# k^T v on both partition halves: ScalarE copies across the halves in place of an exchange by products

## The chip, the core and the metric

One core of a Trainium2 chip runs the whole kernel. The metric is device time in microseconds (us); the kernel before takes 374.31 us, the median of 3 runs (373.65 to 374.38). Engines are named as in the profile: PE is TensorE (PEld its weight loads), ACT is ScalarE, DVE is VectorE, POOL is GpSimd, SP is SyncE, which here only issues DMAs.

## The reference

Two blocks follow each other. The first is linear attention over 8 batches, 8 heads, 576 positions and head size 64:

```python
kv = np.einsum('bhsd,bhse->bhde', k, v)
out = np.einsum('bhsd,bhde->bhse', q, kv)
rms = np.sqrt(np.mean(out * out, axis=-1, keepdims=True) + 1e-06)
attn = (out / rms * g_norm)
x = attn.transpose(0, 2, 1, 3).reshape(4608, 512)
```

The second is a mixture of 8 experts with an early exit: tokens with `x @ w_skip > 0` go to the expert with the largest `x @ w_gate`, which adds `gate * (relu(x @ w1[e]) @ w2[e])` to x; the others leave as they are. Everything is float32.

## The kernel before

**Two stages.** The attention stage (lines 141 to 1057) takes the first 118 us of the profiled execution: it loads q, k and v, makes x, stores it, and works out the routing beside that. The expert stage (from line 1060) takes the rest: each expert's tokens are gathered, and two layers are computed with large products.

**The state of a batch.** For each batch b, `state` (L372) sums k^T v of its 8 heads in PSUM, in 64x64 products (L380) cut into portions over several steps. The heads are numbered 2u+w; those of w=0 stand on partitions 0 to 63 of `sum_ps`, those of w=1 on partitions 64 to 127. Two positions are handled together: q^T has an even position's 64 dimensions on partitions 0 to 63 and an odd position's on 64 to 127. So every head's k^T v must stand in the tile `kvd` twice, once on each half of the partitions, with zeros beside it. The copy on the head's own half is called `own(b, w)`. Each row holds 146 columns (PK): 9 gate columns, 128 columns of k^T v of two heads, 9 gate columns; the gate columns hold k^T v times the gate and skip weights, so that logits come out of the same product as x.

The steps that make `kvd` are:

- the end of `state`: two ACT copies of 64x256 (L387) put k^T v of `sum_ps` on its own half
- `state_t` (L390): four products with the identity (L394) turn it, and one ACT copy (L397) takes the result to `kvT`
- `state_m` (L400): two products (L403) with the gate weights, and two ACT copies of 64x36 (L406) put the gate columns on the own half
- `state_s` (L408), the exchange: two products with the identity (L412), each of which reads one half of `kvd` and writes the other half of PSUM, and two ACT copies of 64x292 (L416) that put all 146 columns of two heads on the other half of `kvd`

A float32 product shows in the profile as two passes, so the exchange is 4 rows of PE in each batch, 32 in all.

**The order.** It is written out by hand: all engines get their instructions in program order. A loop over 36 units and two more steps (L1014) runs, in step n: `turn(n+1)` (transposes of q, L461, and an ACT copy to `qT`, L464), `root(n-1)` (ACT square root, L530), the jobs called "early", `values(n)` (products of q with `kvd`, L499, into a PSUM tile `o_ps`, ahead of them the transposes of a last position, L480; then an ACT square, L515), the jobs "mid", `norm(n-1)` (DVE reciprocal, L537, and DVE product L546, which reads `o_ps` and ends its use), `squares(n)` (DVE sum, L523), and the jobs "pe". From unit 30 on `squares(n)` comes before `norm(n-1)`. The portions of `state` and the three other steps of batch b are such jobs, laid out in L964 to L982: `state_t` in step s, `state_m` in step s too (as "pe", so after `values`), `state_s` in step s+1. For the last batch the places differ somewhat. Batch 0 is done ahead of the loop (L954 to L962).

**What is shared.** `o_ps` has two buffers, so `values(n)` waits until L546 has read unit n-2. `sum_ps` has one, and the next batch's `state` waits until it has been read; units 30 and 33 use its room too. The results of L394, L403 and L412, and the routing's products (L694, L700, L922), lie in one PSUM bank, `g_ps`. Units 16, 17, 34 and 35 (L509) do the ninth position of four batches together.

**Loads.** k, v and q of a batch come in four pieces each (`load_part`, L118), 288 KB a piece, all issued by SP in program order, with stores of x between them. k and v have 3 buffers, q has 2.

Of the kernel before, what the change touches and what calls it, by code (L numbers as in the profile page):

```python
# [17 lines left out]
def kernel(  # L18
# [43 lines left out]
    nc = tc.nc  # L62
    B, H, S, D = q.shape
# [10 lines left out]
    G = E + 1  # L74
# [4 lines left out]
    PK = 2 * KD  # L79

    KVD = 5
# [28 lines left out]
    g_ps = ps_g.tile([P, 512], FP32)  # L110
# [17 lines left out]
    def load_kv(b, js=range(4)):  # L128
        if b < B:
            if js.start == 0:  # L130
                for name, to in (("k", kts), ("v", vts)):
                    to[b] = kv_pool.tile([P, 4, C, D], FP32, tag=name, name=name)
            for j in js:
                for src, t in ((k, kts[b]), (v, vts[b])):
                    load_part(t, src, b, j)

    def load_q(b):
        if b < B:
            qts[b] = load(q_pool, "q", q, b)
# [61 lines left out]
    ident = keep.tile([P, P], FP32)  # L201
# [3 lines left out]
    kvds = []  # L205
# [27 lines left out]
    for a in range(2):  # L233
        r = slice(a * 64, (a + 1) * 64)
# [60 lines left out]
    for lo, m, _ in runs:  # L295
# [26 lines left out]
        out=srow[:, :].rearrange("p (r c) -> p r c", c=CK),  # L322
# [33 lines left out]
    def own(b, w):  # L356

        return kvds[b % KVD][w * 64:(w + 1) * 64, :, w, w, :]

    sum_all = ps_kv.tile([P, 2, 512], FP32, name="sum_ps")  # L360
    sum_ps = sum_all[:, :, 0:2 * D].rearrange("p a (u d) -> p a u d", u=2)
    sw_ps = g_ps[:, 0:2 * PK]
    kvT_ps = g_ps[:, 0:2 * P].rearrange("p (u x) -> p u x", u=2)
    lg_ps = g_ps[:, 2 * PK:2 * PK + 8 * G].rearrange("p (u a w g) -> p u a w g", u=2, a=2, w=2)

    def ends_of(x):

        ap = [list(d) for d in x.ap]
        assert ap[-1] == [1, PK]
        return bass.AP(x.tensor, x.offset, ap[:-1] + [[PK - G, 2], [1, G]])  # L370

    def state(b, some):  # L372

        kt, vt = kts[b], vts[b]
        for i in some:
            u, c = divmod(i, C)
            for w in range(2):
                for a in range(2):
                    r = slice(a * 64, (a + 1) * 64)
                    nc.tensor.matmul(  # L380
                        out=sum_ps[w * 64:(w + 1) * 64, a, u, :],
                        lhsT=kt[r, 2 * u + w, c, :], rhs=vt[r, 2 * u + w, c, :],
                        start=(c == 0), stop=(c == C - 1), skip_group_check=True)
        if some.stop < 2 * C:
            return
        for w in range(2):
            nc.scalar.copy(out=own(b, w)[:, :, G:G + 2 * D].rearrange("p u (a d) -> p a u d", a=2),  # L387
                           in_=sum_ps[w * 64:(w + 1) * 64, :, :, :])

    def state_t(b):  # L390
        for u in range(2):
            for w in range(2):
                r = slice(w * 64, (w + 1) * 64)
                nc.tensor.matmul(out=kvT_ps[:, u, r], lhsT=kvds[b % KVD][:, u, w, w, G:G + 2 * D],  # L394
                                 rhs=ident[:, r], start=True, stop=True)
        kvT = att_pool.tile([P, 2, P], FP32, tag="kvT", name="kvT", bufs=1)
        nc.scalar.copy(out=kvT[:, :, :], in_=kvT_ps)  # L397
        kvTs[b] = kvT

    def state_m(b):  # L400
        kvT = kvTs.pop(b)
        for u in range(2):
            nc.tensor.matmul(out=lg_ps[:, u, :, :, :], lhsT=kvT[:, u, :], rhs=gw_b[:, u, :, :, :],  # L403
                             start=True, stop=True)
        for w in range(2):
            nc.scalar.copy(out=ends_of(own(b, w)), in_=lg_ps[w * 64:(w + 1) * 64, :, :, w, :])  # L406

    def state_s(b):  # L408

        for w in range(2):  # L410
            r, o = slice(w * 64, (w + 1) * 64), slice((1 - w) * 64, (2 - w) * 64)
            nc.tensor.matmul(out=sw_ps[o, :], lhsT=ident[r, r], rhs=own(b, w), start=True, stop=True,  # L412
                             skip_group_check=True)
        for w in range(2):
            o = slice((1 - w) * 64, (2 - w) * 64)
            nc.scalar.copy(out=kvds[b % KVD][o, :, w, 1 - w, :],  # L416
                           in_=sw_ps[o, :].rearrange("p (u k) -> p u k", u=2))


    units = []  # L420
# [22 lines left out]
    def at(step, part, job):  # L443
        todo.setdefault((step, part), []).append(job)
# [7 lines left out]
    def turn(n):  # L452
        _, b, i, u = units[n]
        if i is None:
            qTs[n] = q8s[b][:, u, :, :, :]
            return
        ps = ps_q.tile([P, 2, 2, 2, 64], FP32, tag="q", name="q_ps")
        for w in range(2):
            for hf in range(2):
                c = 4 * i + 2 * hf  # L460
                nc.tensor.transpose(out=ps[:, w, :, hf, :], in_=qts[b][:, 2 * u + w, c:c + 2, :],  # L461
                                    identity=ident[:, :])
        qT = att_pool.tile([P, 2, 2, P], FP32, tag="qT", name="qT")
        nc.scalar.copy(out=qT[:, :, :, :].rearrange("p w a t -> p (w a t)"),  # L464
                       in_=ps[:, :, :, :, :].rearrange("p w a h t -> p (w a h t)"))
        qTs[n] = qT
# [478 lines left out]
    for b in range(KNOWN // S // 4 * 4, KNOWN // S):  # L945
        nc.gpsimd.dma_start(
            out=out[b * S:(b + 1) * S, :].rearrange("(p c) d -> p c d", c=C)[:, C - 1, :],
            in_=zero)

    starts = {}  # L950
    for n, (_, b, i, _) in enumerate(units):
        if i is not None:
            starts.setdefault(b, n)
    state(0, range(C))  # L954
    dense(4)
    state(0, range(C, 2 * C))
    dense(5)
    state_t(0)
    turn(0)
    state_m(0)  # L960
    turn(1)
    state_s(0)  # L962

    portions = {1: (1, (10, 8)), 2: (4, (6, 6, 6)), 3: (7, (5, 6, 7)), 4: (11, (5, 6, 7)),  # L964
                5: (16, (8, 4, 3, 3)), 6: (20, (4, 4, 5, 5)), 7: (24, (4, 4, 5, 5))}
    over = 0
    for b, n in starts.items():
        if b:
            step, counts = portions[b]
            i = 0  # L970
            for count in counts:
                at(step, "early" if step in (starts[1], starts[2], starts[4] - 2) else "pe",
                   lambda b=b, some=range(i, i + count): state(b, some))
                i += count
                step += 1
            assert i == 2 * C and step < n and step - len(counts) > over - 1
            last = b == B - 1
            at(step, "mid" if last else "early", lambda b=b: state_t(b))
            at(*((step + 1, "early") if last else (step, "pe")), lambda b=b: state_m(b))
            at(step + 1, "early" if step + 1 == n else "pe", lambda b=b: state_s(b))  # L980
            over = step
        at(over, "end", lambda b=b: load_kv(b + 3, range(4 if b else 2)))  # L982

        at(n + 2, "end", lambda b=b: load_q(b + 2))
        if b == 0:
            at(n + 2, "end", lambda: load_kv(3, range(2, 4)))
# [73 lines left out]
    with tc.tile_pool(name="wpool_b", bufs=1, reuse_waits="tile") as wpool_b, \  # L1060
# [526 lines left out]
        with tc.If(n_rounds > 1):  # L1587
            with tc.For_i(1, n_rounds, 1):
# [8 lines left out]
                    out=left[:, :].rearrange("p (r c) -> p r c", c=CK),  # L1597
# [39 lines left out]
```

## Time and profile before

| what | value |
|---|---|
| median of 3 runs | 374.31 us |
| profiled execution, its own time | 371.14 us |
| its span in the profile | 369.3 us |
| granted TensorE clock, mean | 0.997 |
| PE busy | 359.9 us (97%) |
| L380, k^T v: PE rows | 1152, 25.3 us |
| L499, q times `kvd`: PE rows of the 128x146 form | 240, 36.0 us |
| L412, exchange: PE rows | 32, median 431 ns |
| L387, k^T v to its own half: ACT rows | 16, median 371 ns |
| L406, gate columns: ACT rows | 16, median 186 ns |
| L416, exchange: ACT rows | 16, median 397 ns |

The profile shows one execution. A row's duration is that of one instruction from start to end; on PE rows overlap, so the distance between starts and not the duration is what a row takes of the engine. A view of the timeline merges neighbouring instructions of one line, and gives start, length and count. The chain of waits is followed back from the last instruction: at each step to what released it, or to the instruction before it on its engine. A wait that names several engines is put down to the one that came last.

### The profile page before, as it was taken

The numbers are of one execution on the slowest core, as the hardware profiler recorded it, in microseconds if no ns is written. First come the engines' busy times: TensorE is split into PE (matmuls) and PEld (weight loads), VectorE is DVE, ScalarE is ACT, GpSimd is POOL, SyncE is SP. The second block draws the span as 40 slices with busy tenths as digits, with TensorE's granted clock in tenths as the row PEclk, the third lists the DMA queues.
The fourth block names the chain that finished last, engine by engine and source line by source line (L and its number), as shares of the span: only waits on it lengthen the run. The fifth ranks groups of instructions, "written<-read, shape, count | busy, mean of one in ns | idle before, by whom it ended". The sixth has DMA issues, their size and how long they took to land.

```text
span 369.3 us, 9717 instructions
## 1 busy us (share of the span) xinstructions
PE 359.9 (97%) x3859; PEld 314.8 (85%) x3859; DVE 242.8 (66%) x630; ACT 146.2 (40%) x398; POOL 118.9 (32%) x189
## 2 busy tenths in 40 slices
PE   8999999899999999999999999999999999999994
PEld 4788998798889769599879988988998988999983
DVE  3355557767878662866847675776776876868831
ACT  2467677666777032134203511421530430441420
POOL 8036466655777072223031303303203202002003
PEclk9999999999999999999999999999999999999998
DMA  8999999999588449973617355564662772601001
GB/s 267 397 390 390 399 397 382 386 379 344 187 296 309 115 129 369 395 234 112 227 56 251 87 208 177 183 231 105 240 230 56 263 244 52 251 3 46 13 1 54
DMA packets 32808, 81.71 MB, mean 221 GB/s; under 512 B 3242, under 2 KB 3250, under 8 KB 32756
## 3 DMA queue, kind: packets, MB, share of 16 engines
q1 hardware_dynamic: 28944, 69.48, 53.0%
q0 software_dynamic: 3792, 11.53, 9.3%
q8 instruction: 32, 0.52, 0.5%
q14 instruction: 20, 0.16, 0.1%
q10 hardware_dynamic: 20, 0.02, 0.0%
HBM read 66.80 MB, written 14.48 MB: 220 GB/s over the span
## 4 chain that ended last, share of the span: by engine, by line
PE 86%; issue 5%; DMA 2%; ACT 2%; DVE 2%; POOL 1%; SPq 0%; POOLq 0%; DVEq 0%; ACTq 0%
PE bank L1261 45%; PE bank L1193 9%; PE o_ps L499 8%; PE sum_ps L380 5%; PE bank L1181 4%; PE q_ps L461 4%; DMA v<-in_v_dram 2%; PE g_ps L394 2%; PE bank L1162 2%; PE g_ps L412 1%; PE o_ps L480 1%; PE g_ps L857 1%; ACT sq L515 1%; PE g_ps L403 1%; PE q_ps L857 1%
## 5 line engine op out<-in xcount | busy, mean ns | idle before, releaser
L1271 ACT COPY p<-bank 128x128 f32<-128x128 f32 (+6 forms) x70 | 20.8, 297 | 99.0 <-PE bank L1261 97.5
L1261 PE MATMUL bank<-xt,w 128*128 128x128 f32 (+5 forms) x336 | 55.5, 288 | 0.0
L1392 POOL DMA_INDIRECT out_dram<-xg,rows x14 | 14.0, 999 | 118.1 <-DVE xg L1389 106.9
L616 POOL TENSOR_TENSOR xb<-xl,g_b 128x512 f32<-128x512 f32 x34 | 41.3, 1215 | 29.2 <-DVE rs L537 27.3
L1261 PEld LDWEIGHTS bank<-xt,w 128*128 128x128 f32 x336 | 47.0, 190 | 1.9 <-DVE bank L1265 1.4
L1265 DVE TENSOR_TENSOR bank<-bank,p 128x128 f32<-128x128 f32 (+6 forms) x70 | 23.6, 337 | 30.3 <-PE bank L1261 29.1
L499 PE MATMUL o_ps<-kvd,qT 128*128 128x146 f32 x240 | 36.0, 290 | 0.9 <-issue 0.7
L1261 PE MATMUL bank<-xs,s 128*128 128x128 f32 (+5 forms) x224 | 36.7, 288 | 0.0
L523 DVE TENSOR_REDUCE rs<-sq 128x8 f32<-128x512 f32 x36 | 24.5, 682 | 14.8 <-ACT sq L515 14.8
L499 PEld LDWEIGHTS o_ps<-kvd,qT 128*128 128x128 f32 x240 | 31.6, 189 | 1.6 <-issue 0.9
L1261 PEld LDWEIGHTS bank<-xs,s 128*128 128x128 f32 x224 | 31.1, 190 | 1.0 <-ACT p L1271 0.8
L1193 PE MATMUL bank<-w,ht 128*32 128x128 f32 (+2 forms) x424 | 29.9, 313 | 0.0
L546 DVE TENSOR_TENSOR xl<-o_ps,rs 128x584 f32<-128x584 f32 x32 | 24.5, 767 | 4.3 <-DVE rs L537 0.5
L1193 PEld LDWEIGHTS bank<-w,ht 128*32 128x32 f32 (+2 forms) x424 | 18.2, 119 | 10.7 <-issue 7.6
L1261 PE MATMUL bank<-t,ht 128*128 128x256 f32 x112 | 27.0, 384 | 0.0
L1261 PE MATMUL bank<-w,ht 128*128 128x256 f32 x112 | 26.5, 380 | 0.0
L515 ACT ACTIVATE sq<-o_ps 128x512 f32<-128x512 f32 x34 | 20.3, 597 | 15.0 <-PE o_ps L499 14.8
L1153 POOL DMA_INDIRECT xg<-out_dram,src x14 | 14.1, 1006 | 35.4 <-DMA out_dram<-xg,rows 18.6
L380 PE MATMUL sum_ps<-v,k 64*64 64x64 f32 x1152 | 25.3, 222 | 0.2 <-DMA v<-in_v_dram 0.2
L1261 PE MATMUL bank<-t,hs 128*128 128x256 f32 x112 | 25.3, 379 | 0.0
L380 PEld LDWEIGHTS sum_ps<-v,k 64*64 64x64 f32 x1152 | 21.6, 134 | 3.6 <-issue 0.9
L1261 PEld LDWEIGHTS bank<-t,ht 128*128 128x128 f32 x112 | 20.8, 190 | 3.9 <-issue 1.2
(224 smaller groups left out, 677.1 us busy)
## 6 DMA issues: line engine op xcount, KB each, us to landing
w<-in_moe_w_dram SPq DMA_DIRECT2D x16, 2048.0 KB, 10.2
k<-in_k_dram SPq DMA_DIRECT2D x32, 288.0 KB, 6.2
v<-in_v_dram SPq DMA_DIRECT2D x32, 288.0 KB, 6.5
q<-in_q_dram SPq DMA_DIRECT2D x32, 288.0 KB, 5.7
out_dram<-xb SPq DMA_DIRECT2D x29, 256.0 KB, 5.5
out_dram<-xb POOLq DMA_DIRECT2D x7, 256.0 KB, 5.9
xg<-out_dram,src POOLq DMA_INDIRECT x16, 3.5
out_dram<-xg,rows POOLq DMA_INDIRECT x16, 6.4
```

What stands on the lines that cost most here:

```text
L380: nc.tensor.matmul(out=sum_ps[w * 64:(w + 1) * 64, a, u, :], lhsT=kt[r, 2 * u + w, c, :], rhs=vt[r, 2 * u + w, c, :], start=(c == 0), stop ...
L461: nc.tensor.transpose(out=ps[:, w, :, hf, :], in_=qts[b][:, 2 * u + w, c:c + 2, :], identity=ident[:, :])
L499: mm = nc.tensor.matmul(out=ps[:, w, 0:2 * PK].rearrange("p (r k) -> p r k", r=2)[:, :, cols], lhsT=qT[:, w, a, :], rhs=kvds[b % KVD][:, u ...
L515: nc.scalar.activation(out=sq[:, :, :, :], in_=heads(ps, G, G + 2 * D), func=ACT.Square)
L523: nc.vector.tensor_reduce(out=rs[:, :, :], in_=sq[:, :, :, :].rearrange("p x y (a d) -> p x (y a) d", a=2), axis=AX.X, op=ALU.add)
L546: nc.vector.tensor_tensor(out=xl[:, :, :, :].rearrange("p x y (a k) -> p x (y a) k", a=2), in0=ps[:, :, 0:2 * PK].rearrange("p x (h k) -> ...
L616: late.append((lambda eng: eng.tensor_tensor(out=xb[:, :, 4 * u * D:(4 * u + 4) * D].rearrange("p r (w x) -> p r w x", w=2), in0=xl[:, :, ...
L1181: nc.tensor.matmul(out=hps[:, cols], lhsT=w_sb[r][0][:, dc, f * P:(f + 1) * P], rhs=xt[:, dc, cols], start=(dc == 0), stop=(dc == DC - 1))
L1193: nc.tensor.matmul(out=yps[q * m:(q + 1) * m, 0:n], lhsT=ht(f)[:, off:off + m], rhs=w_sb[r][1][:, f, q * n:(q + 1) * n], start=(f == 0), s ...
L1261: nc.tensor.matmul(out=out, lhsT=lhsT(i), rhs=rhs(i), start=start and i == 0, stop=i == k - 1, skip_group_check=True)
L1265: nc.vector.tensor_tensor(out=to, in0=x, in1=y, op=ALU.add)
L1271: nc.scalar.copy(out=t, in_=x)
```

## The change

The exchange goes. `own` gets a counterpart `other`, the same heads on the other half of the partitions, and both halves are filled by ACT copies straight out of PSUM; the copies for `other` read one half of the partitions and write the other half.

- The 64x256 copies of k^T v are made twice: for `own` where they were, at the end of `state`; for `other` in `state_t`, behind the copy to `kvT`.
- The 64x36 copies of the gate columns are made twice, both in `state_m`.
- `state_s` with its 2 products and 2 copies of 64x292 is gone from each batch, and so are its jobs.
- `state_m` is a "mid" job now and not a "pe" job (but for the last batch, where it stays "early" of the next step).

```diff
+    def other(b, w):
+        return kvds[b % KVD][(1 - w) * 64:(2 - w) * 64, :, w, 1 - w, :]
+
+    def put_sums(b, half):
+        for w in range(2):
+            nc.scalar.copy(out=half(b, w)[:, :, G:G + 2 * D].rearrange("p u (a d) -> p a u d", a=2),
+                           in_=sum_ps[w * 64:(w + 1) * 64, :, :, :])
...
-    sw_ps = g_ps[:, 0:2 * PK]
...
-        for w in range(2):
-            nc.scalar.copy(out=own(b, w)[:, :, G:G + 2 * D].rearrange("p u (a d) -> p a u d", a=2),
-                           in_=sum_ps[w * 64:(w + 1) * 64, :, :, :])
+        put_sums(b, own)
...
         nc.scalar.copy(out=kvT[:, :, :], in_=kvT_ps)
+        put_sums(b, other)
         kvTs[b] = kvT
...
-        for w in range(2):
-            nc.scalar.copy(out=ends_of(own(b, w)), in_=lg_ps[w * 64:(w + 1) * 64, :, :, w, :])
-
-    def state_s(b):
-        for w in range(2):
-            r, o = slice(w * 64, (w + 1) * 64), slice((1 - w) * 64, (2 - w) * 64)
-            nc.tensor.matmul(out=sw_ps[o, :], lhsT=ident[r, r], rhs=own(b, w), start=True, stop=True,
-                             skip_group_check=True)
-        for w in range(2):
-            o = slice((1 - w) * 64, (2 - w) * 64)
-            nc.scalar.copy(out=kvds[b % KVD][o, :, w, 1 - w, :],
-                           in_=sw_ps[o, :].rearrange("p (u k) -> p u k", u=2))
+        for half in (own, other):
+            for w in range(2):
+                nc.scalar.copy(out=ends_of(half(b, w)), in_=lg_ps[w * 64:(w + 1) * 64, :, :, w, :])
...
-    state_s(0)
...
-            at(*((step + 1, "early") if last else (step, "pe")), lambda b=b: state_m(b))
-            at(step + 1, "early" if step + 1 == n else "pe", lambda b=b: state_s(b))
+            at(*((step + 1, "early") if last else (step, "mid")), lambda b=b: state_m(b))
```

## The prediction

> **What bounds it now.** I read the page first, then busy times by stretch, then the chain of waits through the attention stage, then the timelines of ACT, DVE, PE and SP around one batch.
>
> ```profile
> span 369.3 us, 9717 instructions
> ...
> PE 359.9 (97%) x3859; PEld 314.8 (85%) x3859; DVE 242.8 (66%) x630; ACT 146.2 (40%) x398; POOL 118.9 (32%) x189
> ...
> DMA  8999999999588449973617355564662772601001
> ```
>
> PE is busy throughout, and DMA is full for the first ten slices of 9.2 us: in that time two resources can each hold the other. By stretch (PE, PEld, DVE, ACT, POOL busy; clock; DMA share):
>
> ```profile
> 20.00:30.00 10.00, 9.81 (x213) 8.85 (x203) 5.25 (x10) 5.94 (x16) 4.98 (x10) 1.00 1.05 388
> 40.00:50.00 10.00, 10.00 (x175) 9.23 (x174) 5.04 (x10) 7.62 (x21) 5.77 (x11) 1.00 1.03 394
> 90.00:100.00 10.00, 9.98 (x176) 9.13 (x174) 8.82 (x25) 7.96 (x21) 7.32 (x12) 1.00 0.57 197
> ```
>
> ACT has 2 to 4 us of 10 left; until 90 us the DMA share is at its top. The chain of waits is PE nearly without a break, and the exchange is on it. Batch 2's:
>
> ```profile
> 39.89 0.21 PE g_ps L412
> 40.10 0.17 PE sum_ps L380 x5
> 40.27 0.25 PE g_ps L412 x2
> 40.53 0.70 PE sum_ps L380 x38
> 41.22 0.34 PE o_ps L480 x2
> ```
>
> **Removed from PE.** From 39.89 to 41.22 are 1.33 us, with a portion of 48 passes of L380 in it. Such a portion alone takes 0.86 us in the chain (31.87 to 32.73), so the exchange takes 0.47. In the same way batch 3 gives 1.22 - 40/48 x 0.86 = 0.50, batches 5 and 6 give 1.10 - 0.57 = 0.53 each. Batch 1 gives 1.41 - 0.86 = 0.55, and 0.18 that L412 waits for L406 (27.25 to 27.43): 0.7. Batch 7 has no L380 beside it: 0.64. Batch 0 is followed below. Batch 4's exchange (60.8) lies where the chain runs over DVE, from the square at 59.53 to L546 at 65.61 and L480 at 66.44: nothing is gained there, and nothing lost, since DVE goes through the same work.
>
> **Added to and removed from ACT.** The timeline of ACT for batch 3:
>
> ```profile
> 45.27 0.77 ACT L387 COPY kvd<-sum_ps 64x256 f32<-64x256 f32 x2 [0.16 <-PE sum_ps L380]
> ...
> 47.00 0.37 ACT L397 COPY kvT<-g_ps 128x256 f32<-128x256 f32 x1 [0.16 <-PE g_ps L394]
> 48.12 0.60 ACT L515 ACTIVATE sq<-o_ps 128x512 f32<-128x512 f32 x1 [0.74 <-PE o_ps L499]
> 48.61 0.38 ACT L406 COPY kvd<-g_ps 64x36 f32<-64x36 f32 x2
> 49.02 0.59 ACT L464 COPY qT<-q_ps 128x512 f32<-128x512 f32 x1
> 49.50 0.30 ACT L530 ACTIVATE rs<-rs,eps_t 128x8 f32<-128x8 f32 x1
> 49.90 0.60 ACT L515 ACTIVATE sq<-o_ps 128x512 f32<-128x512 f32 x1
> 50.60 0.82 ACT L416 COPY kvd<-g_ps 64x292 f32<-64x292 f32 x2
> ```
>
> Out goes the pair of 0.82; in come a pair of 64x256 at 0.77 and one of 64x36 at 0.38: +0.33 us of ACT a batch. The copies that cross the halves have no row in the trace. The nearest rows are the same shapes without a crossing, and I take their price; bounds: that price below (nothing in a crossing could make it cheaper), twice it above (read and written as two passes).
>
> Where it lies: the pair of 0.77 starts behind L397 (47.37 to 48.14), just in ACT's idle 0.74 before the square: the square comes 0.02 later. The next batch's `state`, which waits for `sum_ps`, follows L403 on PE; for batch 2 that is 38.49, and the pair is done at 38.31. The two extra 64x36 copies delay everything behind them on ACT by 0.38 unless ACT idles before its next work. It does for batches 2, 5 and 6 (0.76, 0.64, 1.33 us idle before L464), and for batch 4 (0.47 before L530). It does not for batches 1, 3 and 7. There `qT`, the root and then DVE's L546 come later, and for L546 waits `values(n+2)`:
>
> ```profile
> 50.17 0.77 DVE L546 TENSOR_TENSOR xl<-o_ps,rs 128x584 f32<-128x584 f32 x1
> ```
>
> It ends at 50.94; L480 of unit 12, for which it frees the tile, starts at 51.51. With +0.39 it ends at 51.33, and PE, 0.50 ahead, would ask at 51.01: 0.3 of the 0.5 would go back. Batch 1 just fits (L546 of unit 3 at 29.7, asked for at 29.8).
>
> Two rules of the Trainium skill speak here. "Trace analysis" (Perfetto Trace Analysis, section Optimizing Scalar/DVE Operations) says that grouping into larger operations helps if the engine is saturated; this change cuts one copy in two. Were ACT saturated, 8 x 0.33 = 2.6 us would be lost; its rows of 5.94 to 7.96 in 10 say that it isn't, so I count only the places above. And "ScalarE: Activation LUTs" (What ACT_TABLE_LOAD costs) has neighbouring instructions overlap by about 93 ns, with 186 ns + 0.833 ns an element: the two extra 64x36 copies would cost 2 x 0.12 = 0.25. The row shows 0.38 for two, with no overlap; I take the row. The rule would give back 0.14 in each place where these copies count.
>
> **A longer hold on the shared bank.** The routing's L694 lies in `g_ps`, behind `state_m` of batch 6, and waits already (total, times, longest):
>
> ```profile
> PEld g_ps L694 <- ACT kvd L406: 0.2, 1, 0.2
> ```
>
> At 87.68 it follows the end of L406 (87.64). With four copies that is 88.03: PE, which has come to it, loses 0.4. Behind it stand L700, the transposes and `values(25)`. So batch 6 keeps 0.53 - 0.4 = 0.13.
>
> **Batch 0** is serial. ACT: `kvT` ends 13.85, the crossing pair 14.62, `qT` 15.21, the third 64x36 copy 15.8: L499 starts at 15.85, not 16.41: 0.56. **Batch 7**: the same copies push ACT's square of unit 29 from 101.37 (end) to about 101.9; DVE's sum and L902 end at 102.75 and not 102.51, and L922 needs that at 103.03 - 0.64 = 102.39: 0.36 goes back, 0.28 stays.
>
> **What is late next: the loads.** They run in a fixed order at full rate, so they don't come earlier when PE is earlier.
>
> ```profile
> 41.27 2.50 SPq L118 DMA_DIRECT2D q<-in_q_dram  x4
> ```
> ```profile
> 48.22 0.64 PE L461 MATMUL q_ps<-ident,q 128*128 128x128 f32 x4
> 51.51 0.38 PE L480 MATMUL o_ps<-ident,q 128*128 128x128 f32 x2
> ```
>
> These are the four pieces of batch 3's q, and their first use in `turn(12)`, which needs two. Issues stand 0.62 apart, and an issue of L118 lands 6.0 us later (median; 3.0 to 7.5): the second lands near 47.9, against its use at 48.44. By then PE would be 0.4 + 0.7 + 0.47 = 1.57 ahead, at 46.9. It waits; some 0.5 is left. (Batch 0's 0.56 counts as 0.4, since the last piece of batch 1's v, issued at 13.39, lands between 19.9 and 20.7 and is used at 20.74.) The wait also gives L546 of unit 10 time, so batch 3 then keeps its whole 0.5. Later loads are early by 4 us or more (batch 4's q: 53.0 + 6 for 63.7; batch 6's: 78.0 + 6 for 88.3).
>
> **Sum.** 0.5 at 48 us, +0.5 (batch 3), 0 (4), +0.53 (5), +0.13 (6), +0.28 (7) = 1.9 us. From there to the end the chain is PE, weights are fetched as their buffers come free, and all of it moves along. The profiled execution's 371.14 (span 369.3) becomes 369.2. The median of the runs stands 3.17 above that execution; the difference goes on the median: 374.31 - 1.9 = 372.4.
>
> **Rivals.** (A) As worked out: 372.4, own range 371.5 to 373.4; chance 0.48. (B) The loads don't hold PE: for it speaks that PE waited for DMA 0.2 us in all; against, the share of 1.05. Then batch 3 keeps 0.2 and the sum is 1.73 + 0.2 + 0.53 + 0.13 + 0.28 = 2.9, or 371.4; with none of the new waits at all it is 0.56 + 0.7 + 0.47 + 0.5 + 2 x 0.53 + 0.64 = 3.9, or 370.4; chance 0.2. (C) The early gains end in the loads wholly (POOL's stores, earlier too, push q of batch 3 back by up to their 0.66 us each) and the late ones in DVE, busy 8.82 of 10 behind 88 us: about -0.3, 374.0; chance 0.17. (D) Slower: crossing copies cost twice. That puts 0.77 + 0.38 more on ACT in each batch, between `kvT` and the root. For batch 3 L546 would end at 52.5, asked for at 51.0: 1.5 lost against 0.5 gained; over some five batches about +4, and 1.5 back where ACT idles: near 377. It decides from about 1.4 times the straight price, where 0.46 more a batch eats the 1.9. No row speaks for it, none excludes it; chance 0.15.
>
> Numbers: a measurement of this kernel tells about 0.2% (0.75 us) from no change. Faster is A and B, 0.68; same is C, 0.17; slower D, 0.15. The range runs from B's end to a little above C, and leaves out D: 370.3 to 374.8.
>
> **What would show it.** L412 and L416 gone; crossing rows at 371 and 186 ns (twice: D); PE waiting for DMA q about 1 us near 47 us (none: B); L694 waiting 0.4 for ACT; batch 4's stretch unchanged; the last L509 some 1.9 us earlier, and from there every expert step equally early. If the expert stage changes its length, or the gain comes from elsewhere, the sum is wrong even if the time fits.

## The result, and the profile after

After: 374.62 us, median of 14 runs (373.14 to 376.26). Before, beside it on the same chip: 375.18 (373.65 to 376.44, 14 runs). The ratio is 0.999, 95% interval 0.997 to 1.001: no difference that can be told, some 0.4 us less at best guess, where 1.9 us less were forecast.

The two profiled executions can't be subtracted. That of before took 371.14 us, 4 us under the median given here; that of after took 376.26. The page after:

```profile
span 374.5 us, 9664 instructions
...
PE 359.3 (96%) x3827; PEld 315.1 (84%) x3827; DVE 244.9 (65%) x630; ACT 148.8 (40%) x414; POOL 119.0 (32%) x189
```

PE has 32 instructions fewer and ACT 16 more, as the diff says, and ACT is busy 2.6 us longer (8 x 0.33). What I expected of the chain of waits around batch 2 is there: the portion of 48 passes stands alone, with L477 directly behind it.

```profile
40.59 0.86 PE sum_ps L388 x48
41.45 0.34 PE o_ps L477 x2
```

The timeline of ACT for batch 3 shows the new rows (L366 is the pair of 64x256 that crosses the halves, L414 now four copies, two of them crossing):

```profile
47.74 0.37 ACT L403 COPY kvT<-g_ps 128x256 f32<-128x256 f32 x1 [0.16 <-PE g_ps L400]
48.14 0.76 ACT L366 COPY kvd<-sum_ps 64x256 f32<-64x256 f32 x2
...
49.41 0.77 ACT L414 COPY kvd<-g_ps 64x36 f32<-64x36 f32 x4
...
50.80 0.30 ACT L527 ACTIVATE rs<-rs,eps_t 128x8 f32<-128x8 f32 x1
```

0.76 for a crossing pair against 0.77 for the straight one; 0.77 for four small copies against 0.38 for two. Crossing costs nothing: rival D is out. Two waits that I had named are there too (all waits of the run: total, times, longest):

```profile
PEld g_ps L691 <- ACT kvd L414: 0.6, 1, 0.6
...
PE q_ps L458 <- DMA q<-in_q_dram: 0.5, 1, 0.5
```

What I had not named is in the busy times by stretch (PE, PEld, DVE, ACT, POOL; clock; DMA share):

```profile
40.00:50.00 10.00, 9.18 (x160) 8.15 (x160) 5.10 (x10) 7.28 (x22) 5.79 (x11) 1.00 1.03 369
...
102.00:104.00 2.00, 1.01 (x9) 0.82 (x8) 1.87 (x3) 1.72 (x4) 2.00 (x3) 1.00 1.00 342
104.00:106.00 2.00, 1.49 (x29) 1.40 (x29) 1.15 (x5) 0.39 (x2) 0.23 (x2) 0.99 1.02 414
106.00:108.00 2.00, 2.00 (x11) 2.00 (x10) 1.69 (x6) 0.79 (x2) 1.19 (x2) 0.50 0.92 371
108.00:110.00 2.00, 2.00 (x13) 1.99 (x13) 0.80 (x2) 1.43 (x3) 1.48 (x4) 0.65 0.67 201
```

Behind the last batch PE idles for 1.5 us of 4, and then the granted clock is 0.50 and 0.65: 11 and 13 products in 2 us. In the profile of before the clock is 1.00 in all of these stretches. The place is seen in the timelines. Before, VectorE's `bv` starts 0.02 us ahead of a GpSimd product:

```profile
102.27 0.24 DVE L902 TENSOR_TENSOR bv<-ohc,row_k 128x88 bf16<-128x88 bf16 x1
102.29 1.26 POOL L616 TENSOR_TENSOR xb<-xl,g_b 128x512 f32<-128x512 f32 x1
```

After, it starts 0.20 us behind it:

```profile
102.92 1.18 POOL L613 TENSOR_TENSOR xb<-xl,g_b 128x512 f32<-128x512 f32 x1
103.12 1.08 DVE L899 TENSOR_TENSOR bv<-ohc,row_k 128x88 bf16<-128x88 bf16 x1
104.25 0.69 PE L919 MATMUL g_ps<-bv,oha_k 128*128 128x4 bf16 x22 [1.24 <-DVE bv L899]
```

The same operation takes 1.08 us and not 0.24, and ends 0.10 us after GpSimd's product. PE waits 1.24 us for it. The clock of 0.50 then lasts 3.4 us, from 106.0 to 109.4 us of this execution.

**Theories.** T1, called the port race after a page that is cited further down: the square of unit 29 stands later on ACT, as forecast; `bv` so falls behind GpSimd's product, waits for its end, and PE's idle time lets the clock fall in some executions. T2, the loads: what is saved ahead of 48 us ends in the wait for q. T3, the longer ACT queue alone (`qT` of batch 0, root of unit 10, square of unit 29) eats the gain. T4, noise: the profiles differ by their runs.

### The profile page after: what moved, and what is told of

Same layout as the page of the kernel before. It is cut to its first block, busy times and chain, and to the rows that moved or that the text cites. A ratio compares the mean times of both kernels' runs of the same rounds, so it can differ in the third digit from the quotient of the medians.

```text
span 374.5 us, 9664 instructions
## 1 busy us (share of the span) xinstructions
PE 359.3 (96%) x3827; PEld 315.1 (84%) x3827; DVE 244.9 (65%) x630; ACT 148.8 (40%) x414; POOL 119.0 (32%) x189
## 4 chain that ended last, share of the span: by engine, by line
PE 84%; issue 6%; DVE 3%; ACT 3%; DMA 2%; POOL 1%; SPq 0%; POOLq 0%; DVEq 0%; ACTq 0%
PE bank L1256 44%; PE bank L1188 9%; PE o_ps L496 7%; PE sum_ps L388 5%; PE bank L1176 4%; PE q_ps L458 4%; PE q_ps L171 2%; PE g_ps L400 2%; PE bank L1157 2%; DMA q<-in_q_dram 2%; DVE rs L520 1%; DVE xl L543 1%; PE o_ps L477 1%; ACT sq L512 1%; ACT kvd L366 1%
## 5 line engine op out<-in xcount | busy, mean ns | idle before, releaser
L496 PE MATMUL o_ps<-kvd,qT 128*128 128x146 f32 x240 | 36.9, 295 | 0.4 <-issue 0.4
L496 PEld LDWEIGHTS o_ps<-kvd,qT 128*128 128x128 f32 x240 | 32.9, 195 | 0.5 <-issue 0.5
L543 DVE TENSOR_TENSOR xl<-o_ps,rs 128x584 f32<-128x584 f32 x32 | 24.5, 767 | 4.3 <-DVE rs L534 0.5
L388 PE MATMUL sum_ps<-v,k 64*64 64x64 f32 x1152 | 24.2, 228 | 1.5 <-issue 1.5
L388 PEld LDWEIGHTS sum_ps<-v,k 64*64 64x64 f32 x1152 | 20.5, 140 | 5.6 <-issue 3.1
L512 ACT ACTIVATE sq<-o_ps 128x512 f32<-128x512 f32 x34 | 20.3, 598 | 11.3 <-PE o_ps L496 10.9
```

Of the source, the lines that this page charges most:

```text
L388: nc.tensor.matmul(out=sum_ps[w * 64:(w + 1) * 64, a, u, :], lhsT=kt[r, 2 * u + w, c, :], rhs=vt[r, 2 * u + w, c, :], start=(c == 0), stop ...
L496: mm = nc.tensor.matmul(out=ps[:, w, 0:2 * PK].rearrange("p (r k) -> p r k", r=2)[:, :, cols], lhsT=qT[:, w, a, :], rhs=kvds[b % KVD][:, u ...
L512: nc.scalar.activation(out=sq[:, :, :, :], in_=heads(ps, G, G + 2 * D), func=ACT.Square)
L543: nc.vector.tensor_tensor(out=xl[:, :, :, :].rearrange("p x y (a k) -> p x (y a) k", a=2), in0=ps[:, :, 0:2 * PK].rearrange("p x (h k) -> ...
```

## The experiments

The experiments were measured in three sets, each with its own runs of the kernel before, whose medians are 374.49, 372.94 and 374.06 us. So each ratio is to before in the same set, and times of different sets are not subtracted. The first set holds both kernels again, the last batch by products and batch 3's q earlier; the third holds the longer idle, crossing copies for batches 3 to 7 alone and the last two versions; the other experiments are the second.

Where a clock is called low, the mean granted clock of that execution is below 0.9945. One stretch of 3.4 us at 0.50 takes 0.0046 off the mean, which is 0.995 or more without it. In the result above, 6 of the 14 runs after are low (mean 375.5 us, the others 374.1). The mean doesn't tell where the clock fell. Five of the profiled executions are low, and each has one such stretch: behind the last batch in that of after and in that of the longer idle; at 7.6 to 11.1 us, ahead of all that differs between the kernels, in the repeat of before and in the run with the last batch by products; and at 73.5 to 76.9 us in the run with GpSimd's product behind `bv`.

**Both kernels again.** No edit.

> The kernel before again, unchanged, for its granted clocks and a second profile. Loads-and-last-batch theory: median near 375.2, ratio 1.000 within 0.003; in the profile q of batch 3 does not hold PE by more than 0.2 us near 48 us, and the clock stays at 1.00 from 100 to 112 us. Noise theory (the two profiles differ by their run, not by the change): this profile too shows slices of 2 us with a clock below 0.8 behind the last batch, and an expert stage that differs from the first profile's 250.5 us by about 2 us.

> The changed kernel again, unchanged. Loads-and-last-batch theory: ratio 0.997 to 1.001; PE waits for q of batch 3 by 0.4 to 1 us near 49 us, and behind the last batch's copies PE idles over 1 us and the clock falls below 0.8 in a slice of 105 to 111 us. Noise theory: the same ratio, but no wait for q over 0.2 us and a clock of 1.00 there, and the expert stage back at 250.5 us from the first L1176 to the end.

Measured: before 1.0005 (0.9978 to 1.0032); after 0.9991 (0.9970 to 1.0012). Before's new profile shows `bv` at 0.24 us and a clock of 1.00 from 96 to 114 us, but its expert part, from the first transposes of gathered rows (L1162, L1157 after) to the end, takes 236.2 us; the first profile had 234.5, the two of after 236.5 and 236.2. T4 holds for that part: 1.7 us of the gap between the first two pages has nothing to do with the change. It goes with the set, not with the kernel: 236.1 to 236.5 us in all four profiles of this set, 234.5 or 234.6 in all four of the second, 235.5 to 236.7 in the third. Why is not known. After's new profile has no wait for q, but the same stall, with the clock kept:

```profile
104.00:106.00 2.00, 1.39 (x28) 1.30 (x28) 1.15 (x5) 0.48 (x2) 0.22 (x2) 1.00 0.98 389
106.00:108.00 2.00, 2.00 (x19) 2.00 (x18) 1.79 (x6) 1.29 (x3) 1.19 (x2) 1.00 0.97 393
```

19 products in 2 us, where the other execution had 11. `bv` takes 1.09 us, PE's idle is 1.25. So the stall is in both executions, the fall of the clock in one. Below 0.9945 were 9 of these 22 runs (mean 375.5, the others 373.8): with the 14 of the result 15 of 36. Of the 187 runs of before beside all my experiments there were 2, and 2 of 14 in the repeat here. So low clocks go with the changed kernel, but they come in some 4 of 10 runs, and the new profile is of a run without, against my expectation.

**The last batch by products.**

```diff
+    CROSS = (0, 1, 2, 3, 4, 5, 6)
...
-        put_sums(b, other)
+        if b in CROSS:
+            put_sums(b, other)
...
+            if b not in CROSS:
+                at(step + 1, "early" if step + 1 == n else "pe", lambda b=b: state_s(b))
```

> The changed kernel with the last batch's exchange by products, as in the kernel before; batches 0 to 6 by crossing copies. If the longer ACT queue of the last batch costs the loss (PE idle, then a low clock): 1 to 2.5 us faster than the changed kernel, ratio to before 0.993 to 0.997, clock 1.00 from 100 to 112 us. If the loads alone ate the gain: the last batch's gain is lost too, 0 to 0.6 us slower than the changed kernel, ratio 0.999 to 1.002. Noise theory: no difference to the changed kernel within 0.5 us.

Measured 0.9955 (0.9937 to 0.9973), 1.7 us below before, with 3 of 22 clocks low and `bv` at 0.24 us. The changed kernel in the same set is 0.3 us below before, so crossing copies in the last batch cost most of what those of the other seven bring. This speaks against T2 and T4; T1 and T3 both foresee it.

**Batch 3's q earlier.**

```diff
-        at(over, "end", lambda b=b: load_kv(b + 3, range(4 if b else 2)))
+        at(over, "end", lambda b=b: load_kv(b + 3, range(2 if b < 2 else 4)))
...
+        if b == 1:
+            at(n + 2, "end", lambda: load_kv(4, range(2, 4)))
```

> The changed kernel with q of batch 3 loaded ahead of the second half of batch 4's k and v, so about 3 us earlier; all copies as in the changed kernel. If the loads eat the early gain: no wait for q near 49 us, the transposes of unit 12 come 0.5 to 1.4 us earlier, and the time falls by as much, ratio to before 0.995 to 0.998. If other waits (qT of batch 0, L543 of unit 10) eat it: the transposes of unit 12 come less than 0.3 us earlier and the ratio is that of the changed kernel within 0.001.

Measured 1.0006 (0.9981 to 1.0031). No wait for q is left, yet the copy of unit 12's transposes starts at 50.07 us, against 50.31 and 50.39 in the two profiles of after: PE has stood 0.63 us for no cause that the profile shows ("issue", at 44 us) and later 0.24 for L543. 11 of 22 clocks are low. T2 in its strong form, where the wait for q alone eats the early gain, is not borne out. In part the loads do hold PE, but earlier. In the new profile of after, PE waits at 20 us for the last piece of batch 1's v:

```profile
20.93 0.33 PE L388 MATMUL sum_ps<-v,k 64*64 64x64 f32 x4 [0.75 <-DMA v<-in_v_dram]
```

**GpSimd's product behind `bv`.**

```diff
-        nc.vector.tensor_tensor(out=bv[:, :, :, :], ...
+        weighed_1 = nc.vector.tensor_tensor(out=bv[:, :, :, :], ...
...
-            scale(now[0])
+            scale(now[0], weighed_1)
```

> The changed kernel, with GpSimd's second 128x512 product in the last batch (L613, xb of unit 29) made to follow VectorE's bv (L899); nothing else moves. If bv loses the race for SBUF to that product: bv back from 1.09 to 0.24 us, the PE idle before L919 from 1.25 to about 0.4 us, the granted clock at 1.00 there in nearly all runs, and 0.9 to 1.5 us faster than the changed kernel, ratio to before 0.994 to 0.997. If the longer ACT queue alone delays L919: bv stays near 1.09 us or PE's idle stays over 1 us, and the ratio stays at 0.999 within 0.001.

Measured 0.9958 (0.9943 to 0.9974), 1.6 us below before; 1 of 23 clocks low. The timeline is that of the low run. It stands some 3.5 us later from 76 us on: PE idles 1.81 us at 70.7 us ("issue"), and 1.0 us behind that idle time the clock falls to 0.50 for 3.4 us.

```profile
106.72 0.24 DVE L899 TENSOR_TENSOR bv<-ohc,row_k 128x88 bf16<-128x88 bf16 x1
107.01 0.69 PE L919 MATMUL g_ps<-bv,oha_k 128*128 128x4 bf16 x22 [0.39 <-DVE bv L899]
...
107.03 1.19 POOL L613 TENSOR_TENSOR xb<-xl,g_b 128x512 f32<-128x512 f32 x1 [0.48 <-DVE bv L899]
```

ACT's queue is as long as in the changed kernel; only the order of two operations on two other engines differs. T3 alone is out: of PE's 1.24 us, 0.85 go with the order, and 0.39 are left with the queue as it is.

**Filler on PE.** Four products that nothing uses stand where PE idles.

```diff
             scale(now[0])
+            dense(4, ps_q.tile([P, 512], FP32, tag="q", name="q_ps"))
```

> The changed kernel with four filler products of the ones tile (128x512 bf16, about 0.22 us each) on PE ahead of L919, where it idles 1.25 us; they compute nothing that is used. If the idle time starts the fall of the clock: bv stays at 1.09 us, L919 starts when it did, but runs with a mean clock below 0.9945 go from 15 in 36 to at most 3 in 22, and the mean falls by about 0.7 us, ratio to before 0.997 to 0.999. If low clocks come of something else: their share stays near 0.4 and the time is that of the changed kernel or up to 0.3 us more.

Measured 0.9985 (0.9963 to 1.0006); 0 of 14 clocks low.

```profile
102.90 1.02 PE L171 MATMUL q_ps<-ones 128*128 128x512 bf16 x4
...
103.02 1.08 DVE L899 TENSOR_TENSOR bv<-ohc,row_k 128x88 bf16<-128x88 bf16 x1
```

`bv` is as late as in the changed kernel, but the low clocks are gone: at that kernel's rate of 15 in 36, none in 14 would come up once in some 2,000 times. The changed kernel was not run in this set, so the rate is that of the runs before it. The time can't be told from that of the changed kernel or of before; the 0.7 us that I expected is below what these runs resolve.

**`bv` late in the kernel before.** Nothing of the exchange is touched.

```diff
+        nc.vector.tensor_tensor(out=ohc[:, :, :], in0=hi_k[:, 0:NE].unsqueeze(2).to_broadcast([P, NE, 2]),
+                                in1=colid_i[:, 0:2].unsqueeze(1).to_broadcast([P, NE, 2]),
+                                op=ALU.is_equal)
         bv = gat_pool.tile([P, NE, 2, 2], BF16, tag="bv1", name="bv1")
```

> The kernel before, with one small VectorE operation (ohc of 128x44 computed a second time, 0.19 us) directly ahead of bv; the exchange stays on PE. Port-race theory: bv now starts about 0.15 us behind GpSimd's product and takes 1.0 to 1.1 us in place of 0.24; PE idles about 0.9 us more ahead of L922, low clocks appear in some 40 of 100 runs, and the time rises by 0.9 to 1.6 us, ratio 1.002 to 1.005. ACT-queue theory: bv takes 0.24 us and the time rises by 0.2 us at most, ratio 1.000 within 0.001.

Measured 1.0016 (0.9999 to 1.0034); 0 of 22 clocks low.

```profile
103.64 1.21 POOL L616 TENSOR_TENSOR xb<-xl,g_b 128x512 f32<-128x512 f32 x1
103.85 1.12 DVE L905 TENSOR_TENSOR bv<-ohc,row_k 128x88 bf16<-128x88 bf16 x1
...
105.01 0.69 PE L925 MATMUL g_ps<-bv,oha_k 128*128 128x4 bf16 x22 [0.47 <-DVE bv L905]
```

0.21 us too late, and `bv` takes 1.12 us in the old kernel too. The exchange itself still fills PE here, so it idles 0.47 us and not 0.9, and the clock holds: about 0.6 us is lost, less than the 0.9 to 1.6 expected, and the expected low clocks did not come: in 22 runs an idle of 0.47 us brought none.

**A longer idle in the kernel before.** The same line, computed six times (`for _ in range(6)`), holds `bv` up longer.

> The kernel before, with ohc computed six times more ahead of bv, so that PE idles about 1.3 us before L922; the exchange stays on PE and ACT's queue as it was. If the idle time is what lets the clock fall: 30 to 50 of 100 runs have a mean clock below 0.9945 and are some 1.7 us longer than the rest, mean 1.5 to 2.5 us above before, ratio 1.003 to 1.007. If low clocks belong to the crossing copies: all runs at 0.995 or more, and 1.2 to 1.6 us above before, ratio 1.003 to 1.004.

Measured 1.0106 (1.0055 to 1.0158) over 6 runs, 4.0 us above before; 5 of 6 clocks low.

```profile
107.46 0.69 PE L926 MATMUL g_ps<-bv,oha_k 128*128 128x4 bf16 x22 [1.66 <-DVE bv L906]
...
109.50 2.15 PE L499 MATMUL o_ps<-kvd,qT 128*128 128x146 f32 x8
```
```profile
110.00:112.00 2.00, 2.00 (x10) 1.99 (x10) 1.07 (x4) 0.43 (x2) 1.19 (x2) 0.50 0.45 123
```

PE idles 1.66 us, and 2 us later its eight products take 2.15 us, not 1.17, at a clock of 0.50. No crossing copy is in this kernel. Here it is not `bv` that is long (0.25 us) but the six operations ahead of it, which take 2.25 us in place of six times 0.19. The second of them, 0.20 us behind the start of a GpSimd product, takes 1.07 us.

```profile
104.87 2.25 DVE L902 TENSOR_TENSOR ohc<-hi_k,colid_i 128x44 bf16<-128x44 int32 x6
104.90 1.21 POOL L616 TENSOR_TENSOR xb<-xl,g_b 128x512 f32<-128x512 f32 x1
107.16 0.25 DVE L906 TENSOR_TENSOR bv<-ohc,row_k 128x88 bf16<-128x88 bf16 x1
```

Idle of 0.47, 1.25 and 1.66 us at this place goes with low clocks in 0 of 22, 15 of 36 and 5 of 6 runs. That the loss came out above my 1.5 to 2.5 us fits the longer idle and the more frequent fall.

**Crossing copies for some batches.** As in the diff above, with `CROSS = (0, 1, 2)`; and with `CROSS = (3, 4, 5, 6, 7)` and GpSimd's product behind `bv`.

> Crossing copies for batches 0 to 2 alone; batches 3 to 7 exchange by products as before. If the loads hold PE at 48 us: 0 to 0.6 us faster than before, ratio 0.998 to 1.000, and PE waits for q of batch 3 before the transposes of unit 12. If they don't: 1.2 to 1.7 us faster, ratio 0.995 to 0.997, and no such wait over 0.2 us. The last batch shows bv at 0.24 us either way.

> Crossing copies for batches 3 to 7 alone, with GpSimd's product behind bv; batches 0 to 2 exchange by products. By the segments of the earlier profiles (0.22 us batch 3, 0.45 batch 5, 0.04 batch 6, 0.29 batch 7) 1.0 us faster than before, ratio 0.996 to 0.998. If the late gains vanish into waits of the loads and the instruction supply: within 0.4 us of before, ratio 0.999 to 1.001.

Measured: batches 0 to 2 alone 0.9968 (0.9952 to 0.9984), 1.2 us below before, and in the profile no wait for q, but 0.41 us for v at 20 us; batches 3 to 7 alone 0.9976 (0.9953 to 0.9999), 0.9 us below. No low clock in 22 runs of either. The first lies nearer to what follows if the loads do not hold PE, though its interval (0.6 to 1.8 us) touches the other case; the second is as the segments said.

**`bv` behind `ohc`**, and the same with batch 0's crossing pair behind `qT`, as a version that might beat both.

```diff
                                 op=ALU.is_equal)
-        yield
         bv = gat_pool.tile([P, NE, 2, 2], BF16, tag="bv1", name="bv1")
...
                                 op=ALU.mult)
+        yield
         ps = g_ps[:, GB:GB + 4]
```

> The changed kernel with bv computed directly behind ohc, one step earlier on VectorE, so neither the square of unit 29 nor GpSimd's product stands ahead of it. Port-race theory: PE goes from unit 30's products to L919 with no wait, low clocks at most 2 in 22, and the time is 1.3 to 2.0 us below the changed kernel, ratio to before 0.993 to 0.997. ACT-queue theory: the wait moves to the next use of unit 29's square, and at most 0.4 us is gained, ratio 0.998 to 1.000.

> As the kernel with bv behind ohc, and in batch 0 the crossing pair of 64x256 stands behind unit 0's qT copy on ACT, so that the second transposes do not wait 0.75 us for that copy. All theories: the wait of L458 for qT near 16 us falls to below 0.2 us, unit 0's products still wait for the last gate copy, and the time changes by 0 to 0.4 us; ratio to before 0.992 to 0.997.

Measured 0.9964 (0.9935 to 0.9994) and 0.9962 (0.9939 to 0.9985). In the first, `bv` needs 0.25 us at 100.64, and L919 follows unit 30's products without a wait, as the port race foresees. The time is yet only about 1 us below the changed kernel, not the 1.3 to 2.0 that I expected. In the second the wait for `qT` near 16 us is gone, and unit 0's products wait 0.51 us for the last gate copy; it changes nothing that can be told. I expected at most 2 low clocks in 22 and got 3 in 16 and 6 in 22: with this place mended they still come. A place is at hand, though not shown: in the profiles of these two PE waits 0.9 and 1.2 us in all, at 109 to 112 us, for gathered rows of the expert stage, once for 1.00 us in one piece; in neither of the two did the clock fall. Neither version is better than the simpler one with GpSimd's product behind `bv`. That one and the one with the last batch by products are each faster than the kernel before, by 1.6 and 1.7 us, their intervals ending 0.3% below it.

## Why the prediction was wrong, step by step

The starts of ACT's squares (L515, L512 after) mark the units; the two profiles of before give 11.31 us each from unit 11 to 15, for example. Units 27 and 35 enclose what follows the last batch's copies; they stand as follows in before, in the new profile of after (its clock at 1.00), and with GpSimd's product behind `bv`:

```profile
95.49 0.60 ACT L515 ACTIVATE sq<-o_ps 128x512 f32<-128x512 f32 x1 [0.50 <-PE o_ps L499]
...
113.22 0.60 ACT L515 ACTIVATE sq<-o_ps 128x512 f32<-128x512 f32 x1
```
```profile
96.20 0.60 ACT L512 ACTIVATE sq<-o_ps 128x512 f32<-128x512 f32 x1 [0.49 <-PE o_ps L496]
...
114.47 0.60 ACT L512 ACTIVATE sq<-o_ps 128x512 f32<-128x512 f32 x1
```
```profile
99.71 0.60 ACT L512 ACTIVATE sq<-o_ps 128x512 f32<-128x512 f32 x1 [0.50 <-PE o_ps L496]
...
117.15 0.60 ACT L512 ACTIVATE sq<-o_ps 128x512 f32<-128x512 f32 x1
```

- **Crossing copies at the straight price**: right (0.76 and 0.77 us).
- **0.5 us at 48 us, since the loads hold PE**: too small. Batches 0 to 2 alone bring 1.2 us (0.6 to 1.8), against 0.5 by my wait and 1.57 without it. I took the landing times of one execution for fixed. The wait for q is in 3 of 9 profiles with these copies early (0.46, 0.21, 1.26 us), one of the other six having q loaded earlier. The loads hold PE more often at 20 us, at batch 1's v, for which I had taken off 0.16 us: in 7 of the 9 profiles PE waits there, 0.19 to 1.37 us, and in none of the five without these copies. PE also comes later by stalls marked "issue" at 24 and 44 us. The kernel before has these too: 0.50 and 1.36 us in its second profile, none over 0.2 at these places in the one I read. Of the terms, batch 1's 0.7 can be read by itself and is right: from unit 3 to 7 all nine profiles take 11.04 to 11.06 us, the five others 11.78 to 11.97. Rival B, the loads not holding PE, was nearer in size; what it says of them is not so at 20 us.
- **Batch 3, 0.5**: 0.28 and 0.21 (11.03 and 11.10 us for 11.31), about the 0.2 that I gave for no wait for q. **Batch 4, 0**: not readable; an "issue" stall of 0.3 to 1.8 us lies in it in each profile.
- **Batch 5, 0.53**: 0.46 (11.19 us twice from unit 19 to 23, before 11.65 twice). **Batch 6, 0.13**: 0.04; PE stands 0.47 or 0.48 us ahead of L691, where I had 0.4.
- **Batch 7, 0.28 saved**: this is the step that failed. From unit 27 to 35 before takes 17.73 and 17.74 us, after 18.27 in the execution with the clock at 1.00: 0.54 lost. I had the square of unit 29 come 0.5 us later relative to unit 28, and so it does (3.45 us for 2.95). I then gave `bv` its old 0.24 us behind it. It had started 0.02 us ahead of a GpSimd product; moved back, it meets it. With the order mended, PE waits 0.39 us for the queue, where I had 0.36, and the segment takes 17.44 us: 0.29 saved, my 0.28. So it is the price of `bv` alone that I had wrong here, 1.08 us for 0.24.
- **"From there all of it moves along"**: right for the 21.6 us from unit 35 to the first transposes of gathered rows (L1162, L1157 after), the same in all profiles to 0.02 us. Ahead of it the clock did not stay: behind PE's idle time of 1.25 us it is low in 15 of 36 runs, and those took about 1.55 us more, which is 0.65 us on average over all. (3.4 us at half the clock would cost a PE without a break 1.7 us, by my estimate.) In the first profile after, units 27 to 35 take 20.27 us. My prediction had no such term.

Sum with the measured terms: -1.2 - 0.2 - 0.46 - 0.04 + 0.54 + 0.65 = -0.7 us; measured -0.4 (-1.1 to +0.4). The sum is rough, since its terms come of different sets and of single profiles. The last batch turned from -0.28 to about +1.2. That the time lies within my range is luck of a kind: of the cases, "all gains lost" named the size with another mechanism.

One rule would have told: the Trainium skill, "SBUF — State Buffer" (Who interferes with whom), says that a VectorE instruction with two SBUF inputs contends with a GpSimd instruction that reads SBUF, that the ports they share are under an exclusive lock, and that the order of issue decides who waits. `bv` has two such inputs (`ohc`, `row_k`); the rows 0.24, 1.08 and 1.12 us agree, and the row that I costed it by showed the winner's price alone.

**What stays open.** Batches 0 to 2 and 3 to 7 bring 1.2 and 0.9 us apart, together with the same mended order 1.6 (1.0 to 2.1). Whether 0.5 us is lost between them or the intervals only differ isn't settled. Nor is what PE waits for in the "issue" stalls, nor what makes an idle time of some 1.2 us end in a low clock in one execution and not in the next. That the race is for a port of SBUF rests on the page cited; the runs show the order, the length of the wait and that changing the order removes it.

## What to carry to other kernels

When a change moves an operation by a few tenths of a microsecond, look on the other engines for what starts within that distance of it: a row shows the price of the order that was, not of the order that comes. Where PE is the bound, an idle time of it can be charged twice, by its length and by the clock behind it; so put beside each other two or three executions, and their granted clocks, before a difference of profiles is given a cause.

## What the runs showed of the hardware

- A VectorE product of 128x88 (bf16) beside a GpSimd product of 128x512: 0.24 us when it started 0.02 us ahead, 1.08 to 1.12 us when it started 0.20 or 0.21 us behind; it then ended 0.10 to 0.12 us after GpSimd's. The GpSimd product took 1.26 us behind it, against 1.18 when it came first.
- The clock fell to 0.50 for 3.4 us after PE had idled 1.24, 1.66 and 1.81 us in one piece, 1.0 to 1.9 us behind the end of that idle time; after 1.25, 1.36 and 1.54 us it did not in other profiles, and with 0.47 us ahead of the products that read `bv` no clock was low (22 runs). The Trainium skill, "TensorE: Matmul & The Clock Gate" (HAM oscillation — how this bites in real kernels), warns of gaps over about 3.4 us; here gaps about half as long and shorter were enough in part of the executions.
- ACT copies from one half of the partitions to the other took 0.37 or 0.38 us (64x256) and 0.19 us (64x36), as those that stay within a half.
